# S4 convolution, router and gate on one core: kernel at 641 times, spectrum by constant matmul, order by a list

## The chip, the cores and the metric

The kernel runs on one core of a Trainium2 chip. Times are microseconds (us) of device time for one execution, and a quoted time is the median of the executions of that kernel. An execution counts as slow here when it is more than 1.5% above the fastest of its kernel. The profile of a kernel is one execution with the hardware profiler on, and its span is a little shorter than the device time. Engines: PE is TensorE's matmul, PEld its weight load, DVE is VectorE, ACT is ScalarE, POOL is GpSimd, SP is SyncE, whose queue issues most DMAs. "Clock" is the share of full speed that TensorE's clock was granted.

## The reference, cut to what matters

```python
xn = layernorm(u)                                    # [1, 2048, 512]
# S4 convolution: one kernel of 2048 taps for each of 512 channels, 128 states each
l = jnp.arange(L).astype(bfloat16)                   # <- the times are rounded
P = jnp.exp(logdA[:, :, None] * l[None, None, :])
K = jnp.einsum("dn,dnl,dn->dl", Cc, P, dB).real
y = irfft(rfft(pad(xn)) * rfft(pad(K)))[:2048] + xn * Dskip
# gate: a router picks the ONE row with the largest xn @ w_r; an FFN updates that row only
g = silu(xn + scatter(ffn(xn[row]) * sigmoid(r[row])))
out = u + y * g
```

Two facts carry the change. First, the times are rounded to bf16: 0 to 256 are exact, and each of the three octaves above has 128 values, so only 257 + 3 x 128 = 641 of the 2048 times are distinct. Second, the FFT has length 4096 and its inputs are real.

## The kernel before: the parts that matter

Its parts follow each other in the source order of a hand-written program, with hand-placed semaphore waits. The kernel K is made from powers: 65 small steps and 32 large ones for every channel, two matmuls a channel, 1024 in all, each with a 65-wide result.

```python
# 8 groups of 64 channels: sines, powers, then one matmul pair per channel
for j in range(32):
    ...
    K.op(PE, lambda t, ...: t.matmul(o_ap, lhsT=gr[:, :, dd], rhs=qr[:, :, dd], start=True, stop=False, ...
    K.op(PE, lambda t, ...: t.matmul(o_ap, lhsT=gi[:, :, dd], rhs=qi[:, :, dd], start=False, stop=True, ...
# a transposing copy on ScalarE, 16 of them
src = KT[32 * gp:32 * gp + 32, :, :].transpose([0, 2, 1])
dst = KTN[32 * q:32 * q + 32, :, 32 * gp:32 * gp + 32]
K.op(AC, lambda a, src=src, dst=dst: a.activation(out=dst, in_=src, func=ACT.Copy), sig="ktn")
```

Then K goes through the same two-stage FFT as the input, in four quarters of 128 channels. Each quarter multiplies spectra with four real products and combines them on GpSimd, inverts in two stages, and each stage change goes through DRAM.

```python
for oi, (ia, ib) in enumerate([(0, 2), (1, 3), (0, 3), (1, 2)]):
    K.op(DV, ... v.tensor_tensor(out=tb[:, oi, :], in0=ub[:, ia, :], in1=ub[:, ib, :], op=ALU.mult), ...
K.op(PO, ... g_.tensor_tensor(out=Y[:, 0, kg, :], in0=tb[:, 0, :], in1=tb[:, 1, :], op=ALU.subtract))
K.op(PO, ... g_.tensor_tensor(out=Y[:, 1, kg, :], in0=tb[:, 2, :], in1=tb[:, 3, :], op=ALU.add), sig="y")
...
for q in range(NQ):
    st_s2(q)
    st_ia(q)
    st_cd(q)
    ...
```

## Time and profile before

The time before is 629.4 us (median of four executions, 621.1 to 630.0).

The page of the profile before: the span, each engine's busy time with its share and instruction count, then 40 equal slices of the span with the busy tenths of VectorE, the granted clock and the DMA share.

```profile
span 620.8 us, 9925 instructions
PE 248.1 (40%) x3915; PEld 173.6 (28%) x3915; DVE 421.6 (68%) x1135; ACT 271.6 (44%) x405; POOL 54.3 (9%) x132
...
DVE  0989516599999899899973012709609659698725
...
PEclk9999975555755567566566555555555555555555
DMA  9920000010000000000000090499169979979293
```

No engine is full over the whole span, but VectorE is at 7 or more in most slices of the first half. The slices show phases in series: one that VectorE fills, one (slices 23 to 25) where VectorE nearly stops, and one where DMA is near 9 and VectorE swings between 0 and 9.

The same by stretch: start and end, length, busy time of the five engines (and their instruction counts), clock, DMA share, GB/s. The stretches are start, making K, gate, spectrum with inverse.

```profile
0.00:123.00 123.00, 22.06 (x215) 11.23 (x215) 73.37 (x196) 7.75 (x30) 0.20 (x4) 0.85 0.28 83
123.00:354.00 231.00, 97.82 (x1096) 66.45 (x1096) 191.05 (x515) 154.91 (x202) 0.00 (x0) 0.58 0.02 5
354.00:391.00 37.00, 1.91 (x32) 1.70 (x32) 7.08 (x15) 36.62 (x46) 0.00 (x0) 0.50 0.41 57
391.00:621.00 230.00, 126.27 (x2572) 94.17 (x2572) 150.14 (x409) 72.29 (x128) 54.11 (x128) 0.50 0.79 157
```

Making K holds VectorE for 191 of 231 us. The gate is ScalarE's alone, 36.6 of 37 us. The last stretch needs no engine for more than 150 of its 230 us: its quarters hand over from engine to engine and through DRAM.

The costliest groups of the kernel before: line, engine, operation, output and input, shapes, count, then busy time in us and the mean of one in ns.

```profile
L839 DVE TENSOR_TENSOR T<-UKB 128x128 bf16<-128x128 bf16 x256 | 65.1, 322 | 39.4 <-ACT UKB L831 38.2
...
L672 ACT ACTIVATE KTN<-KT 32x2080 bf16<-32x2080 bf16 x16 | 61.3, 3832 | 0.4
...
L883 DVE CAST C<-PB 128x512 bf16<-128x512 f32 x64 | 39.8, 684 | 18.7 <-PE PB L875 18.7
```

These are the products, the transposing copies and the evictions of the inverse's first stage, 166 us of two engines. The change removes or shrinks all three.

### The profile page before, as it was taken

To read this page: it belongs to the slowest core of one execution; us is meant where nothing else is said; L and a number is where in the kernel's file an instruction comes from. 1 tells how busy PE (TensorE), PEld (TensorE's weight loads), DVE (VectorE), ACT (ScalarE), POOL (GpSimd) and SP (SyncE) were. 2 spreads that over 40 slices of the span, in tenths; PEclk is the share of its full clock that TensorE was granted. 3 is DMA by queue.
4 is the path that set the end of the run, shared out by engine and by line. 5 is a ranking of instruction groups with operands and counts; after the bars stand their busy time and mean duration, and the time that the engine had idled before them with its cause. 6 is when DMAs were issued, how large, how long until landed. Compare 5 with 4: busy or idle time off the path is not lost.

```text
span 620.8 us, 9925 instructions
## 1 busy us (share of the span) xinstructions
PE 248.1 (40%) x3915; PEld 173.6 (28%) x3915; DVE 421.6 (68%) x1135; ACT 271.6 (44%) x405; POOL 54.3 (9%) x132
## 2 busy tenths in 40 slices
PE   0000361142632455275075010775485595534401
PEld 0000220100532224055054010773283383322201
DVE  0989516599999899899973012709609659698725
ACT  0000011374528866974962999755055055023000
POOL 0000000000000000000000000007107107126000
PEclk9999975555755567566566555555555555555555
DMA  9920000010000000000000090499169979979293
GB/s 235 366 51 0 0 1 1 3 68 0 2 0 1 1 1 1 1 2 1 1 1 1 3 133 0 113 227 183 24 186 177 184 191 186 196 195 122 119 150 71
DMA packets 93743, 49.57 MB, mean 80 GB/s; under 512 B 86688, under 2 KB 90624, under 8 KB 91776
## 3 DMA queue, kind: packets, MB, share of 16 engines
q1 hardware_dynamic: 89744, 40.50, 33.4%
q10 hardware_dynamic: 3952, 8.44, 4.1%
q8 instruction: 31, 0.51, 0.4%
q14 instruction: 16, 0.13, 0.1%
HBM read 27.96 MB, written 18.87 MB: 75 GB/s over the span
## 4 chain that ended last, share of the span: by engine, by line
DVE 31%; ACT 19%; PE 16%; issue 8%; DMA 6%; SPq 0%; POOL 0%; DVEq 0%; ACTq 0%; POOLq 0%
DVE T L839 9%; ACT KTN L672 7%; DVE C L883 6%; PE PB L775 6%; PE PB L650 3%; PE PB L652 3%; DMA D<-scr_c 2%; DVE TT L623 2%; ACT QR L556 2%; DVE EBF L570 2%; ACT QI L555 2%; DVE TT L624 2%; PE PB L867 2%; ACT PB L731 1%; ACT G L734 1%
## 5 line engine op out<-in xcount | busy, mean ns | idle before, releaser
L839 DVE TENSOR_TENSOR T<-UKB 128x128 bf16<-128x128 bf16 x256 | 65.1, 322 | 39.4 <-ACT UKB L831 38.2
L650 PE MATMUL PB<-QR,GG 128*32 128x65 bf16 x512 | 61.0, 297 | 34.9 <-DVE GG L627 34.9
L844 POOL TENSOR_TENSOR Y<-T 128x128 bf16<-128x128 bf16 x64 | 29.7, 463 | 516.0 <-DVE T L839 516.0
L550 PE MATMUL PB<-IDI,GAT 64*128 64x512 bf16 (+1 forms) x72 | 36.5, 527 | 91.2 <-ACT QR L556 78.3
L831 ACT ACTIVATE UKB<-PB 128x512 bf16<-128x512 f32 x64 | 37.7, 597 | 56.0 <-DVE T L839 30.3
L672 ACT ACTIVATE KTN<-KT 32x2080 bf16<-32x2080 bf16 x16 | 61.3, 3832 | 0.4
L652 PE MATMUL PB<-QI,GG 128*32 128x65 bf16 x512 | 60.8, 295 | 0.0
L781 ACT ACTIVATE A<-PB 128x512 bf16<-128x512 f32 x64 | 34.6, 614 | 49.0 <-PE PB L775 46.0
L883 DVE CAST C<-PB 128x512 bf16<-128x512 f32 x64 | 39.8, 684 | 18.7 <-PE PB L875 18.7
L664 ACT ACTIVATE KT<-PB 64x455 bf16<-64x455 f32 (+1 forms) x40 | 20.5, 512 | 71.6 <-PE PB L652 71.6
L825 PE MATMUL PB<-B,F 128*32 128x128 bf16 x1024 | 40.1, 307 | 27.1 <-ACT UKB L831 27.0
L556 ACT ACTIVATE QR<-PB,CONSTF 128x512 bf16<-128x512 f32 (+1 forms) x72 | 50.0, 710 | 0.0
L650 PEld LDWEIGHTS PB<-QR,GG 128*32 128x32 bf16 x512 | 37.1, 138 | 35.8 <-DVE GG L627 35.6
L555 ACT ACTIVATE QI<-PB 128x512 bf16<-128x512 f32 (+1 forms) x72 | 43.9, 610 | 4.0 <-PE PB L550 3.9
L570 DVE TENSOR_TENSOR EBF<-EBF,PIV 128x64 bf16<-128x64 bf16 (+5 forms) x48 | 41.2, 859 | 1.7
L550 PEld LDWEIGHTS PB<-IDI,GAT 64*128 64x128 bf16 x72 | 6.6, 100 | 121.4 <-ACT QR L556 107.3
L421 ACT ACT_TABLE_LOAD x1 | 1.3, 1283 | 84.7 <-DVE FT L419 84.7
L867 PE MATMUL PB<-Y,FA 32*128 32x128 bf16 x256 | 25.0, 297 | 31.9 <-DVE C L883 15.7
L652 PEld LDWEIGHTS PB<-QI,GG 128*32 128x32 bf16 x512 | 37.4, 140 | 0.0
L775 PE MATMUL PB<-XZN,CONSTB 32*64 32x128 bf16 x256 | 15.1, 309 | 54.2 <-DMA XZN<-XN 31.8
L825 PEld LDWEIGHTS PB<-B,F 128*32 128x32 bf16 x1024 | 24.8, 129 | 42.1 <-ACT UKB L831 40.8
L775 PE MATMUL PB<-KTN,CONSTB 32*64 32x128 bf16 x544 | 35.2, 308 | 0.5 <-ACT A L781 0.5
(158 smaller groups left out, 524.3 us busy)
## 6 DMA issues: line engine op xcount, KB each, us to landing
scr_a<-A SPq DMA_DIRECT2D x8, 1024.0 KB, 6.7
scr_c<-C SPq DMA_DIRECT2D x4, 2048.0 KB, 8.1
D<-scr_c SPq DMA_DIRECT2D x8, 1024.0 KB, 12.3
B<-scr_a SPq DMA_DIRECT2D x16, 264.0 KB, 4.9
B<-scr_a SPq DMA_DIRECT2D x16, 248.0 KB, 5.8
XZN<-XN SPq DMA_DIRECT2D x16, 128.0 KB, 3.8
out_dram<-X SPq DMA_DIRECT2D x16, 128.0 KB, 3.6
WG<-in_B_w_gate_dram ACTq DMA_DIRECT2D x1, 1376.0 KB, 20.0
```

The lines of the kernel that those rows point to most:

```text
L550: K.op(PE, lambda t, bank=bank, h=h, q=q, i0=i0, n=n: t.matmul(bank[:, 0:64 * n], lhsT=GAT[64 * h:64 * h + 64, q, :], rhs=IDI[64 * h:64 * ...
L555: K.op(AC, lambda a, src=src, i0=i0, n=n, qi=qi: a.activation(out=qi[:, i0:i0 + n, :], in_=src, func=ACT.Sin, scale=-1.0))
L556: K.op(AC, lambda a, src=src, i0=i0, n=n, qr=qr: a.activation(out=qr[:, i0:i0 + n, :], in_=src, func=ACT.Sin, bias=CF[:, 0:1]), sig="arguse")
L570: K.op(DV, lambda v, m=m, lv=lv: v.tensor_tensor(out=EBF[:, m:2 * m, :], in0=EBF[:, 0:m, :], in1=PIV[:, lv:lv + 1, :].to_broadcast([128, m ...
L650: K.op(PE, lambda t, o_ap=o_ap, gr=gr, qr=qr, dd=dd, gp=gp: t.matmul(o_ap, lhsT=gr[:, :, dd], rhs=qr[:, :, dd], start=True, stop=False, ti ...
L652: K.op(PE, lambda t, o_ap=o_ap, gi=gi, qi=qi, dd=dd, gp=gp: t.matmul(o_ap, lhsT=gi[:, :, dd], rhs=qi[:, :, dd], start=False, stop=True, ti ...
L672: K.op(AC, lambda a, src=src, dst=dst: a.activation(out=dst, in_=src, func=ACT.Copy), sig="ktn")
L775: K.op(PE, lambda t_, o_ap=o_ap, lhsT=lhsT, rhs=rhs, q=q, l1=l1, mi=mi, nm=len(mms): t_.matmul(o_ap, lhsT=lhsT, rhs=rhs, start=(mi == 0), ...
L825: K.op(PE, lambda t_, o_ap=o_ap, k2=k2, ro=ro, t=t, m=m, g=g: t_.matmul(o_ap, lhsT=F2[:, k2, 32 * ro:32 * ro + 32], rhs=Bt[t][par][:, m, : ...
L831: K.op(AC, lambda a_, bank=bank, kg=kg: a_.activation(out=UKB[kg % 2][:], in_=bank[:, 0:512].rearrange("p (a b) -> p a b", a=4), func=ACT. ...
L839: K.op(DV, lambda v, ub=ub, tb=tb, oi=oi, ia=ia, ib=ib: v.tensor_tensor(out=tb[:, oi, :], in0=ub[:, ia, :], in1=ub[:, ib, :], op=ALU.mult) ...
L883: K.op(DV, lambda v, g=g, kb=kb: v.tensor_copy(out=Ct[:, 16 * kb + g:16 * kb + 16:4, :], in_=PB[g][:, 0:512].rearrange("p (a b) -> p a b", ...
```

## The change

The intent has four parts.

1. **K only where it differs.** 20 large and 33 small steps for each channel cover the 641 times, so the matmuls are 33 wide instead of 65 and VectorE makes far fewer powers.
2. **Spectrum by constant matmul.** K at 640 times is five blocks of 128 rows. One constant array W, 5.2 MB, holds the sum over equal times and the transform together: 20 full-array matmuls for each group of four frequency blocks take the place of K's two-stage FFT. Time 2048, which the last four taps round to, touches only the last outputs and is added separately.
3. **Products completed in the inverse.** VectorE multiplies the input's spectrum U by K's, and a copy of U with real and imaginary halves swapped (U2S, made by DMA) by K's. The sums and signs of the complex product sit in the constants FA of the inverse. Four products and two GpSimd operations become two products, each eight times wider.
4. **Scheduled by list.** Every operation is a node with its reads, writes and an assumed duration. The builder finds dependencies from memory and banks, in the order in which nodes were created, then a list scheduler fixes each engine's order by longest remaining path. Every engine runs its fixed order.

Cut to its core (`-` before, `+` after, `...` where lines are left out; nearly the whole file is replaced):

```diff
-        for oi, (ia, ib) in enumerate([(0, 2), (1, 3), (0, 3), (1, 2)]):
-            K.op(DV, ... v.tensor_tensor(out=tb[:, oi, :], in0=ub[:, ia, :], in1=ub[:, ib, :], op=ALU.mult) ...
-        K.op(PO, ... subtract)
-        K.op(PO, ... add)
+        def spec(h, tg):                        # h: half of the channels, tg: 8 groups of 4 blocks
+            for t4 in range(4):
+                ...
+                for k in range(5):
+                    mms.append((o, W[:, t, k, :], KT2[:, h, k, :], k == 0, k == 4))
+            ...
+            g.A(lambda e: e.activation(out=ko, in_=sv, func=ACT.Copy), [ko], [sv], 1024)
+            us = (U2[:, h, 4 * tg:4 * tg + 4, :], U2S[h][:, 4 * tg:4 * tg + 4, :])
+            for x in range(2):
+                g.V(... e.tensor_tensor(out=po, in0=us[x], in1=ko, op=ALU.mult), [po], [us[x], ko], 1024, 2)
+            ...
+                    mms.append((o, FA[:, t, x, :], PAB[:, pp, x, t4, :], x == 0, x == 1))
...
+        W = place("W", [128, 32, 5, 128], BF16, o_u)               # on top of X0, AT, BT of the input FFT
+        FA = place("FA", [128, 32, 2, 128], BF16, o_u + 40960)
+        WG = place("WG", [128, 4, FF], BF16, o_u2)                 # FFN weights, on top of U2
...
+        def exps(c, after):                     # exponent arguments of part c (0..7) of K
+            src = args(0, c, c % 2)             # c % 2: PSUM banks 0,1 or banks 2,3
...
+                    bk = (2, 3, 6)[pk % 3]      # input FFT, first stage: banks 2, 3 and 6
...
+    def M(self, mms, **kw):                     # a group of matmuls as one node
+            ns += max(58.0, nn / 2.0)           # assumed duration of each
+    def dma(self, eng, pairs, **kw):
+        return self.add(eng, fns, outs, ins, 60.0 * len(pairs) + 1.3 * nd, dma=True, ...)
+    def schedule(self): ...
+            cand = [n for n in avail[e] if ready[n.i] <= t]
+            n = max(cand, key=lambda n: n.bl + n.bias)
```

## The prediction

> **What bounds the kernel now.** The page gives a span of 620.8 us: VectorE (DVE) 421.6 us busy, ScalarE 271.6, TensorE 248.1. The busy slices and the chain of waits show four phases in series. (1) 0 to 123 us: loads, layernorm, router, parameters, nearly one dependent DVE chain. (2) 123 to 354: generating the S4 kernel at 65 points, DVE about 92% busy (70.8 and 73.4 of 80 us in the table by stretch), with one stall per column quarter for the 32x2080 copies (16 x 3.83 us, ScalarE, 7% of the chain). (3) 354 to 391: the gate on ScalarE with eight reloads of activation tables at 1.28 us. (4) 391 to 621: four quarters of FFT, product, inverse, about 46 us each, in lock step; DVE works 256 products of 322 ns (65 us) and 64 evictions of 684 ns (40 us), DMA moves 256-byte packets at about 190 GB/s with 95% share, and the granted clock is 0.50.
>
> **What the change does, costed from the groups by shape.** DVE bf16 tensor_tensor: 0.29 / 0.42 / 0.69 / 1.22 us for 256 / 512 / 1024 / 2048 elements; from PSUM or in f32, 512 elements 0.69; ScalarE about 1.04 us for 1024 (estimate between 0.61 at 512 and 1.91 at 2048).
> - DVE, estimated: parameters 33, layernorm with bn_stats 26, router and gate 22, qgen 8 x 3.2 = 26, gchain 4 x 12.6 = 50, products 32 x 0.69 = 22, skip and tail 23. About 200 us against 422.
> - ScalarE: about 145 us. The KTN copies and most table loads go, and evictions become 1024 wide.
> - TensorE: 1024 small kernel matmuls at 40 to 60 ns (before: 60 ns each, 61 us for 1024), 320 + 128 full-array N=256 matmuls for the spectrum and the inverse, about 250 others. About 170 us. The Trainium skill, "TensorE: Matmul & The Clock Gate", Part 1, says a sustained burst of some 3.4 us raises the clock from 1.2 to 2.4 GHz; this trace agrees in so far as the clock drops to 0.50 in sparse stretches and reaches only 0.63 in generation bursts. I expect the dense spectrum phase mostly warm: 28 matmuls x 110 ns, 3.1 us a step, 16 steps, 50 us; cold would add about 40.
> - DMA: 7.3 MB of new constants and a 4 MB swap copy; they wait until the input FFT frees its buffers. "DMA: Bandwidth & Descriptors", Specifications, gives about 358 GB/s per core from HBM; the trace shows 358 at 10 to 30 us. At 300, about 38 us, mostly hidden under generation.
> - The list schedule overlaps layernorm, FFT and router with generation.
>
> **Critical path.** Start 10 us; DVE work before the second half's K: about 157 us, plus 5 to 10% gaps and semaphores; last kernel matmuls and the turn through DRAM 18: K complete near 205. TensorE between 150 and 245 carries the last generation (31), the gate (10) and both halves' spectra (50), so the last inverse ends near 245. Last turn through DRAM 13, tail 9, store 5: about 268 us.
>
> **Predicted: 268 us, 80% range 238 to 305.** Faster by over 2%: 0.98; within: 0.01; slower: 0.01.
>
> **What would show it.** DVE about 200 us busy and above 80% in slices up to about 190 us; no 3.8 us copies; granted clock near 1 in the spectrum phase; spectrum steps 3 to 4 us; constants landed before 165 us; last 25 us DMA turn and tail.
>
> **What would make it wrong.** A cold clock in the spectrum phase (+20 to 40); the static order of the list missing real durations, so engines stall behind waits (+30); constants or swap copies late because buffers overlay (+20); generation finishing sooner through better overlap (-25).

## The result, and the profile after

The time after is 304.85 us, median of four executions (303.2, 299.18, and two slow by the rule above, 306.54 and 306.49). Ratios in this text are the mean time of one kernel's fast runs over that of the other's of the same rounds, so not quite the ratio of the medians. Here it is 0.480, with a 95% interval of 0.474 to 0.487; the interval is wide because only two executions are fast. The kernel is 2.1 times as fast. The prediction had the direction, and its centre of 268 us was 37 us too low. The result lies inside the range by 0.15 us (304.85 against 305): its two slow executions, 306.5, lie outside, and the mean of its two fast ones is 301.2. That it fell inside is in part luck.

The page of the profile after, the same lines as before.

```profile
span 301.4 us, 4934 instructions
PE 159.4 (53%) x2067; PEld 98.3 (33%) x2067; DVE 171.7 (57%) x437; ACT 141.5 (47%) x158; POOL 0.2 (0%) x4
...
DVE  1699599999999992479650000030144446356073
...
PEclk9999999999995555855875799659789999975555
DMA  8999700000000002086899959999856649837925
```

VectorE works for 172 us instead of 422, and that is 28 us less than predicted. Yet the span is longer than predicted, so the loss is in waiting. VectorE's slices 22 to 28 (158 to 211 us) are almost empty, while DMA is mostly at 9. Read the clock row with care at the start: in this trace it has no record before 84.6 us (79.4 in the kernel before) and then shows full speed. But matmuls of 256 columns at 23.8, 41.9 and 46.2 us come 213 ns apart, against 109 ns at 87.5 us, so TensorE ran at about half speed there, and the 1.00 of the first stretch below is not a measurement.

The stretches of the kernel after, the same columns.

```profile
0.00:75.00 75.00, 17.98 (x92) 9.03 (x92) 62.69 (x192) 26.32 (x32) 0.20 (x4) 1.00 0.52 125
75.00:140.00 65.00, 33.14 (x754) 19.87 (x754) 53.06 (x148) 42.20 (x55) 0.00 (x0) 0.68 0.18 64
140.00:187.00 47.00, 28.40 (x634) 20.46 (x634) 12.84 (x26) 29.66 (x29) 0.00 (x0) 0.79 0.98 216
187.00:215.00 28.00, 14.41 (x86) 9.89 (x85) 2.88 (x5) 8.39 (x8) 0.00 (x0) 0.74 1.00 255
215.00:269.00 54.00, 50.97 (x375) 35.75 (x375) 24.34 (x39) 34.80 (x35) 0.00 (x0) 0.91 0.66 156
269.00:301.40 32.40, 14.49 (x132) 3.29 (x128) 15.88 (x30) 0.15 (x1) 0.00 (x0) 0.55 0.69 146
```

From 140 to 215 us no engine is busy for more than 43 of 75 us, and the DMA share is about 1. Before that, from 75 to 140, the DMA stands almost still at 0.18. The transfers came late and all at once.

What became of the costly groups: the products are 32 operations of about 690 ns (the sixteen that read U are shown, the others read the swap copies); the transposing copies are gone, and what replaces them is a strided eviction, KT; the kernel matmuls are still 1024, as before, but half as wide.

```profile
L1037 DVE TENSOR_TENSOR PAB<-U_50,K2T 128x1024 bf16<-128x1024 bf16 x16 | 11.1, 692 | 57.2 <-PE PB L184 37.0
...
L184 PE MATMUL PB<-QQ,GG 128*20 128x33 bf16 x1024 | 20.5, 249 | 17.0 <-DVE GG L764 9.3
L805 ACT ACTIVATE KT<-PB 128x264 bf16<-128x264 f32 x16 | 21.7, 1355 | 14.9 <-PE PB L184 14.4
```

The chain that ended last, followed back from the end (start us, length us, engine and what it did), cut to the pieces that tell the story; all matmuls of the kernel after carry the line of one helper, L184, so they are told apart by their operands.

```profile
139.56 3.85 DMA scr_a<-AT
...
148.15 13.55 DMA BT<-scr_a
...
187.04 27.97 DMA FA<-c_fa
215.06 38.99 PE PB L184 x308
...
276.74 10.04 DMA DD_117<-scr_z
```

Read it from the bottom. The dense spectrum phase starts at 215.06, when the constants FA land after 28 us under way. FA was issued at 187.04, because its memory was the input FFT's buffer BT, and the last matmul that reads BT starts at 186.7. BT was loaded late because AT, the first stage's result, was complete only at 139.56. And AT is late for a reason that its own history shows. The evictions of that stage (count, min/median/max ns, first and last start in us):

```profile
L971 ACT ACTIVATE AT<-PB x32: 572/597/932, 50.3 to 138.9; 128x512 bf16<-128x512 f32 x32
```

32 evictions of 0.6 us need 19 us of ScalarE; they were spread over 89 us, though the normalized input was complete at about 74. ScalarE in that time, in order (start, busy us, line, operation, count, idle before and its releaser):

```profile
70.96 0.60 ACT L971 ACTIVATE AT<-PB 128x512 bf16<-128x512 f32 x1 [6.97 <-DVE XN_49 L867]
82.84 2.80 ACT L805 ACTIVATE KT<-PB 128x264 bf16<-128x264 f32 x2 [11.29 <-PE PB L184]
...
99.92 1.94 ACT L697 ACTIVATE EE<-PB 128x1024 bf16<-128x1024 f32 x2 [4.79 <-PE PB L184]
...
108.31 1.41 ACT L971 ACTIVATE AT<-PB 128x512 bf16<-128x512 f32 x2
```

ScalarE had time: it idled 11.3 us at one place. But between 71.6 and 108.3 it evicted nothing of the FFT. The exponentials (EE) of the second half of K stand in between. They read their arguments from PSUM, half of them from banks 2 and 3; the FFT's first stage comes later in the source and writes banks 2 and 3, so it had to wait for them, and they in turn wait for the sines of the first half, so that activation tables change seldom. The count fits: in the source the stage's first 16 groups of matmuls take banks 2, 3 and 6 in turn, so five of them write bank 6, and five evictions, no more, came by 71.6 us. Theory: this bank order, not any engine's work, delays the FFT, and through the shared memory the constants.

### The profile page after: what moved, and what is told of

The parts are those of the page before. It is cut to its first block, busy times and chain, and to the rows that moved or that the text cites. A ratio compares the mean times of both kernels' runs of the same rounds, so it can differ in the third digit from the quotient of the medians.

```text
span 301.4 us, 4934 instructions
## 1 busy us (share of the span) xinstructions
PE 159.4 (53%) x2067; PEld 98.3 (33%) x2067; DVE 171.7 (57%) x437; ACT 141.5 (47%) x158; POOL 0.2 (0%) x4
## 4 chain that ended last, share of the span: by engine, by line
DVE 30%; PE 29%; DMA 21%; ACT 12%; SPq 4%; issue 2%; ACTq 0%
PE PB L184 29%; DMA FA<-c_fa 9%; DVE TT L760 5%; DMA BT<-scr_a 4%; SPq L198 4%; DMA DD_117<-scr_z 3%; DVE JNK L874 3%; DMA LD_66<-in_A_log_dt_dram 3%; ACT EE L697 2%; ACT U_50 L997 2%; DVE QQ L719 2%; DVE QQ L718 2%; DVE GG L762 2%; ACT AT L971 1%; DVE GG L764 1%
## 5 line engine op out<-in xcount | busy, mean ns | idle before, releaser
L184 PE MATMUL PB<-XN_49,CB 32*64 32x512 bf16 (+1 forms) x97 | 29.2, 549 | 39.1 <-ACT AT L971 22.0
L184 PE MATMUL PB<-KT_51,W 128*128 128x256 bf16 x320 | 42.3, 294 | 7.9 <-ACT K2T L1033 5.7
L184 PE MATMUL PB<-CB,AD 128*128 128x256 bf16 (+1 forms) x96 | 19.3, 362 | 38.6 <-DVE AD L650 21.7
L184 PEld LDWEIGHTS PB<-KT_51,W 128*128 128x128 bf16 x320 | 33.2, 105 | 15.3 <-ACT K2T L1033 6.6
L971 ACT ACTIVATE AT<-PB 128x512 bf16<-128x512 f32 x32 | 18.1, 632 | 28.4 <-DVE XN_49 L867 17.5
L184 PE MATMUL PB<-QQ,GG 128*20 128x33 bf16 x1024 | 20.5, 249 | 17.0 <-DVE GG L764 9.3
L805 ACT ACTIVATE KT<-PB 128x264 bf16<-128x264 f32 x16 | 21.7, 1355 | 14.9 <-PE PB L184 14.4
L1033 ACT ACTIVATE K2T<-PB 128x1024 bf16<-128x1024 f32 x16 | 16.2, 1022 | 20.2 <-PE PB L184 11.2
L1047 ACT ACTIVATE ZT<-PB 128x1024 bf16<-128x1024 f32 x16 | 16.4, 1024 | 18.0 <-PE PB L184 16.5
L184 PEld LDWEIGHTS PB<-CB,AD 128*128 128x128 bf16 x96 | 9.6, 130 | 46.3 <-DVE AD L650 21.9
L184 PEld LDWEIGHTS PB<-QQ,GG 128*20 128x20 bf16 x1024 | 17.7, 125 | 20.6 <-DVE GG L764 10.1
L184 PEld LDWEIGHTS PB<-XN_49,CB 32*64 32x64 bf16 (+1 forms) x97 | 6.3, 114 | 55.1 <-ACT AT L971 28.4
L184 PE MATMUL PB<-PAB,FA 128*128 128x256 bf16 x128 | 19.2, 300 | 6.2 <-DMA FA<-c_fa 5.7
L760 DVE TENSOR_TENSOR TT<-GG,ZB 128x512 bf16<-128x512 bf16 (+2 forms) x48 | 21.6, 485 | 0.3
L184 PEld LDWEIGHTS PB<-PAB,FA 128*128 128x128 bf16 x128 | 13.0, 106 | 10.4 <-DMA FA<-c_fa 6.0
L184 PE MATMUL PB<-BT,F2T 128*128 128x256 bf16 (+1 forms) x70 | 10.7, 306 | 10.1 <-DMA BT<-scr_a 6.5
L859 DVE BATCH_NORM_STATS2 ST<-X_78 128x6 f32<-128x512 bf16 x16 | 10.7, 686 | 5.6 <-DMA X_78<-in_A_u_dram 5.5
## 6 DMA issues: line engine op xcount, KB each, us to landing
W<-c_w ACTq DMA_DIRECT2D x4, 1280.0 KB, 11.3
```

What stands on the lines that cost most here:

```text
L184: fns.append(lambda e, o=o, l=l, r=r, st=st, sp=sp, tp=tp: e.matmul(o, lhsT=l, rhs=r, start=st, stop=sp, tile_position=tp, skip_group_chec ...
L760: g.V(lambda e, zb=zb, o=o: e.tensor_tensor(out=o, in0=src, in1=zb, op=ALU.mult), [o], [src, zs], 256 * m, 2)
L805: g.A(lambda e, src=src, dst=dst: e.activation(out=dst, in_=src, func=ACT.Copy), [dst], [src], 264)
L859: g.V(lambda e, b=b: e.bn_stats(ST[:, b, :], X0[:, b, :]), [ST[:, b, :]], [X0[:, b, :]], 512)
L971: g.A(lambda e, o=o, bk=bk: e.activation(out=o, in_=PB[:, bk, :], func=ACT.Copy), [o], [PB[:, bk, :]], 512)
L1033: g.A(lambda e: e.activation(out=ko, in_=sv, func=ACT.Copy), [ko], [sv], 1024)
```

## The experiments

The rival theories were: (B) the bank order; (C) the list's assumed durations are wrong, so its order is poor (by its formula each issue of a quarter of W, 5120 runs at 1.3 ns, holds ScalarE for 6.7 us, and that of FA for 10.7, while the trace shows 0.3 to 1.1 us for ScalarE's issues of W and FA); (F) the layout is at fault, because FA sits on the memory that is freed last; (S) the swap copies crowd FA out; (W) less work, not order, is what matters. Kernels ran beside runs of the kernel before, 629 to 630 us each time; the kernel after was not timed again, and is compared through the ratios. Its own ratio is uncertain by 1.3%, since only two of its executions are fast, so a gain of 2 to 4% over it (e2, e3, e4) is known to about one point only. Every run below is correct except where said, and the times are medians of four executions.

### e1: the exponent arguments of the second half on banks 0 and 1 only

```diff
-            src = args(0, c, c % 2)
+            src = args(0, c, c % 2 if c < 4 else 0)
```

> One edit: the second half's exponent arguments all use PSUM banks 0 and 1, so banks 2 and 3, in which the input FFT's first stage is also written, are free from about 45 us. Theory (a false bank dependency made the input side late: in the changed kernel those exponentials end at 102 us, the first-stage evictions run from 108 to 139 us, and FA therefore lands only at 215 us): first-stage evictions end before 90 us, FA lands at least 20 us earlier than 215, time 270 to 285 us against 303. Rival A (TensorE's fixed order, blocked behind generation and the router, made it late, whatever the banks): evictions still end after 120 us, time within 8 us of 303. Rival B (the constants and the swap copy are simply too many bytes once they start): the evictions end early but FA's landing follows by less than 10 us, time above 293.

Measured: 260.7 us, ratio 0.413 (0.410 to 0.415). That is 14% below the kernel after, and below the range that theory B gave, so its size was underestimated. The same view of the evictions, and three pieces of the chain of waits of this kernel:

```profile
L971 ACT ACTIVATE AT<-PB x32: 588/652/740, 43.3 to 61.8; 128x512 bf16<-128x512 f32 x32
```

```profile
107.03 5.84 PE PB L184 x15
...
152.78 12.95 DMA U2S<-U
...
166.51 17.14 PE PB L184 x140
```

The evictions now take 19 us instead of 89 and end 77 us earlier. FA is issued at 146.7 instead of 187.0 and takes 9.4 us instead of 28.0. Work is unchanged (VectorE 172.4 us, TensorE 165.2). The gain is smaller than 77 us because other things then come last: the second stage of the FFT starts at 115.4, behind the FFN in TensorE's fixed order (the piece at 107.03 holds the FFN's last matmuls). By the source the stage's output U2 lies on the FFN's weights, and every second group of it writes banks 6 and 7, of which the router and the FFN use 7 too; which of the two overlaps put the FFN first no run separates. Then the inverse waits for the swap copy of U2.

### e2: other durations in the list, most of them nearer to the trace

```diff
-            ns += max(58.0, nn / 2.0)
+            ns += max(22.0, nn / 2.0)
...
-        return self.add(eng, fns, outs, ins, 60.0 * len(pairs) + 1.3 * nd, dma=True, ...)
+        return self.add(eng, fns, outs, ins, 450.0 * len(pairs), dma=True, ...)
...
-                g.A(... func=ACT.Copy), [dst], [src], 264)
+                g.A(... func=ACT.Copy), [dst], [src], 1200)
```

> Only the durations that the list scheduler works with are corrected to measured ones: a DMA issue 0.45 us per copy instead of up to 13 us for the constants, the strided kernel eviction 1.35 us class, a small kernel matmul 22 ns instead of 58. The work itself is the same. Theory (false bank dependency first, wrong durations second): first-stage evictions still cannot use banks 2 and 3 before about 100 us, FA lands between 200 and 215, the gate moves out of the last 45 us, time 288 to 300. Rival A (wrong durations in the list are the main cause of the missed estimate): time below 280.

Measured: 290.5 us, ratio 0.462 (0.460 to 0.464). Theory C is worth about 4% (0.4617 over 0.4803), as expected, and is not the main cause: the evictions still end at 126.5 us and FA lands at 194, a little before the expected 200 to 215. The new durations are not nearer to the trace throughout: a group of four loads of BT counts 1.8 us where the old list had 5.6, and the trace of the kernel after has 21 us for eight loads, about 10.5 for four.

### e3: FA on the memory that is freed first

```diff
-        W = place("W", [128, 32, 5, 128], BF16, o_u)
-        FA = place("FA", [128, 32, 2, 128], BF16, o_u + 40960)
+        FA = place("FA", [128, 32, 2, 128], BF16, o_u)
+        W = place("W", [128, 32, 5, 128], BF16, o_u + 16384)
```

(and FA's load is listed before W's)

> FA takes the memory that is free first (that of the first FFT stage), W moves behind it and is loaded by quarters as before. Nothing else changes. Theory (the last wait before the dense spectrum phase is FA, because it lies on the memory that the input FFT frees last): FA lands before 180 us, the first inverse starts near 195 to 205 instead of 215 when the first quarter of W and the swap copy are there, time 285 to 297. Rival (the phase is paced by the bytes of W, FA and the swap together): the first inverse still starts after 210, time 298 to 306.

Measured: 294.5 us, ratio 0.468 (0.466 to 0.469). FA is issued at 143.1, 44 us earlier, and the first inverse starts at 194.1 instead of 215.1. But the time falls only by some 8 us. A write-back of the first half's result (scr_z, 203.6 to 217.7) held the chain for 14 us before the last inverse, which ends at 253 instead of 268; and gate steps, which run from 247 to 270, were left for after it, so that from there to the end it takes 40.4 us instead of 33.4. The layout is worth 3%, and is not the main cause.

### e4: no swap copies (wrong)

```diff
-        for h in range(2):
-            g.dma(SP, [(U2S[h][0:64, :, :], U2[64:128, h, :, :]), (U2S[h][64:128, :, :], U2[0:64, h, :, :])])
...
-            us = (U2[:, h, 4 * tg:4 * tg + 4, :], U2S[h][:, 4 * tg:4 * tg + 4, :])
+            us = (U2[:, h, 4 * tg:4 * tg + 4, :], U2[:, h, 4 * tg:4 * tg + 4, :])
```

> Wrong result on purpose: the 4 MB on-chip copy that swaps real and imaginary halves is left out and the second product reads the unswapped spectrum, so the output is wrong. The rest is the same, in a newly listed order. Theory (FA starts at 187 because its memory comes free then, and takes 28 us for 2 MB because it shares the DMA engines with the copy and with the kernel's turn through DRAM): FA takes 12 to 18 us, lands near 200 to 205, time 288 to 296. Rival B (bytes set the time): time below 285. Rival C (the swap copy costs nothing): time within 4 us of 303.

Measured: 295.5 us, ratio 0.469 (0.467 to 0.470); the result is wrong, as intended (relative error 0.030). FA is still issued at 185.1, but without the copies it needs 10.3 us to land, less than the expected 12 to 18 (kernel, DMA, count, KB, median us to landing):

```profile
FA<-c_fa ACTq DMA_DIRECT2D x1, 2048.0 KB, 10.3
```

So 18 of FA's 28 us went with the copies. This agrees with the Trainium skill, "DMA: Bandwidth & Descriptors", Issuing engines are not separate DMA queues: transfers started by different engines run on the same 16 DMA engines and interleave. FA was issued by ScalarE, the copies by SyncE. Leaving the copies out saves only 2%: the lateness of the issue stays.

### e5: each engine in source order

```diff
-            cand = [n for n in avail[e] if ready[n.i] <= t]
-            n = max(cand, key=lambda n: n.bl + n.bias)
+            n = next(n for n in avail[e] if n.i == seqs[e][len(self.order[e])])
```

> The same instructions as the changed kernel, but every engine issues them in the order in which the program text makes them, instead of the list's order (the waits are derived in the same way). It parts the gain of the change into less work and overlap. Theory (both matter: the work of VectorE fell from 422 to 172 us, and the list overlaps the input side with generation): 370 to 430 us, clearly faster than 629 and clearly slower than 303. Rival A (the gain is nearly all less work, the list's order adds little): below 330. Rival B (without the overlap there is little gain): above 500.

Measured: 434.9 us, ratio 0.690 (0.688 to 0.693), a little above the theory's range.

```profile
PE 186.2 (43%) x2067; PEld 106.5 (25%) x2067; DVE 183.3 (42%) x437; ACT 140.4 (32%) x157; POOL 0.2 (0%) x4
```

The same operations in source order keep no engine busy for half of the time. Against this order, 629 - 435 = 194 us of the gain come from less work, and some 130 us (435 to 305) from the list. That split holds for this one source order, which nobody wrote to be run as it stands.

### e6: e1 and e2 together

> The bank edit of the first experiment together with the corrected durations of the second. Theory (after the bank edit the rest of the lag is order: in the run with the bank edit six of the eight gate steps run alone between 210 and 235 us after the last full spectrum steps, and the FFN holds up the input's second stage until 107 us): the gates move into gaps, time 240 to 252 against 260. Rival (the corrected durations only matter while the bank dependency is there, or not at all): 256 to 264.

Measured: 267.4 us, ratio 0.425 (0.422 to 0.427): slower than e1 alone by 7 us, and outside every range given. A step of my reasoning failed: two changes that each help did not add. The chain shows what it met:

```profile
135.82 22.14 DMA U2S<-U
```

The new durations brought W, FA and both swap copies under way at once. In this kernel a quarter of W takes 19.3 us in the median and FA 15.3 (7.1 and 9.4 in e1); the swap copy that the first inverse waits for takes 22.1, against 12.95 in e1. But that copy landed at 158.0, earlier than the 165.7 of e1, so contention alone does not explain the loss. TensorE, in fixed order, stood before the gate's first matmuls until 159.3, because VectorE had queued a copy that they need behind a product that waited for the swap copy; then 15 us of gate and spectrum matmuls came ahead of the first inverse, which started at 174.1, not 166.5. The last inverse is later by as much (234.2 against 226.6). That order and contention together make the 7 us is argued from these waits; no run shows either alone.

### e7: e1, e2 and e3 together

> The sixth run's edits and FA in the memory that is free first. Theory: after the bank edit FA is issued at 147 us and no matmul waits for it any more; what the first inverse waits for is the swap copy (landing at 166 us). So FA in front gains less than the 8 us that it gained alone: 236 to 248, within 6 us of the sixth run. Rival (FA still is the last wait): 10 us or more below the sixth run.

Measured: 254.2 us, ratio 0.404 (0.402 to 0.406). 13 us below e6, which meets the rival's mark of 10 or more: with the bank order gone, FA's place matters more than it did alone. FA is issued at 74.1 and out of the way of the others: a swap copy takes 12.7 us in the median instead of 19.0, a quarter of W 8.0 instead of 19.3. The range for the theory was missed by 6 us at its upper end. The second stage of the FFT starts its first group at 98.0, the second only at 110.8 and the third at 123.5, with the FFN's products (103.7 to 122.0) among them, and the last inverse ends at 220.5.

### e8: e7, and the router with the FFN ahead in the list

```diff
+        g.boost = 60000.0            # added to the rank of each node until it is set back
         for b in range(16):
             g.V(lambda e, b=b: e.tensor_tensor_reduce(out=JNK[:], in0=XN0[:, b, :], in1=WRB[:], ...
...
+        g.boost = 0.0
         gchain(0)
```

> The seventh run's edits, and the router's and FFN's instructions get a higher priority in the list, since the FFN's weights lie where the input spectrum U2 goes. Theory (after the bank edit the input's second stage waits from about 86 us, when its data is there, to 107 us for the FFN): the second stage starts before 95 us and the time falls to 225 to 240. Rival (generation of the second half, bound by VectorE, is by then the last wait): second stage earlier, but time within 3 us of the seventh run.

Measured: 248.2 us, ratio 0.394 (0.394 to 0.395), the fastest. The FFN's update is ready at 87.6 instead of 124.7 us. The second stage starts at 96.6 instead of 98.0 (before 95 was expected), its third group at 100.2 instead of 123.5, but its eighth at 127.2 instead of 135.3: most of the lead is lost on the way. The total falls by 6 us: less than the theory gave, and more than the rival's 3. In TensorE's order, kernel matmuls that wait for VectorE until 93.3 now stand before the second stage, and more matmuls of K, with waits for ScalarE, among its later groups (idle 1.1 to 3.3 us at a time). So the making of K, and no longer the FFN, seems to hold it; no run tests that.

### e9: the bank order removed by the other side

From the kernel after; the FFT's first stage leaves banks 2 and 3, and the exponentials stay where they were:

```diff
-                    bk = (2, 3, 6)[pk % 3]
+                    bk = 6
```

> A second, different way to remove the same false dependency: the second half's exponents stay on banks 2 and 3 as in the changed kernel, and the input FFT's first stage instead writes only bank 6, one bank without rotation. Theory (the shared banks 2 and 3 are the cause): the first-stage evictions end before 105 us although they now have one bank instead of three, and the time is 262 to 280. Rival (the gain of the first experiment came from some other effect of the new listing): evictions still end after 125 us, time above 292.

Measured: 274.7 us, ratio 0.435 (0.433 to 0.437). The evictions end just past the expected 105:

```profile
L971 ACT ACTIVATE AT<-PB x32: 569/597/947, 41.6 to 105.1; 128x512 bf16<-128x512 f32 x32
```

Two of three banks were taken away from the stage, and the kernel is 9% faster than after. A shortage of banks or of ScalarE could not do that; an order between users of banks 2 and 3 can. With one bank each matmul waits for the eviction before it, so the evictions take longer than in e1 and gain less. This is the second, independent route to theory B.

### e10: e8, and the gate's steps ahead in the list

```diff
+        g.boost = 20000.0
         for k in range(8):
             gate_step(k)
+        g.boost = 0.0
```

> The eighth run's edits, and the gate steps get a higher priority. In the eighth run six of eight gate steps fall after the last spectrum product (203 to 222 us), between inverses that run at the cold rate, 1.9 us instead of 1.04 for eight matmuls. Theory (the late gates hold the last inverses and so the last turn through DRAM): the last inverse ends 5 to 9 us earlier than at 215.6, time 238 to 244 against 248. Rival (the gates only use time that is needed anyway, moving them early pushes the spectrum back by as much): within 2 us of 248.

Measured: 254.4 us, ratio 0.403 (0.401 to 0.405): slower than e8 by 6 us. The theory fell. SyncE's queue in both kernels, e10 first (start, us, line, DMA, count):

```profile
219.93 1.87 SPq L199 DMA_DIRECT2D out_dram<-XR  x4
221.89 0.42 SPq L199 DMA_DIRECT2D scr_z<-ZT  x1
224.17 1.84 SPq L199 DMA_DIRECT2D out_dram<-XR  x4
226.42 4.32 SPq L199 DMA_DIRECT2D DD<-scr_z  x4
```

```profile
219.76 4.00 SPq L199 DMA_DIRECT2D DD<-scr_z  x4
228.15 15.61 SPq L199 DMA_DIRECT2D out_dram<-XR  x16
```

The load DD, on which the end depends, is issued 6.7 us later. About 3 us of that is the spectrum itself: its last inverse is at 218.8 us, against 215.6 in e8, because the gates now stand among its steps. The rest is the queue: with the gates done early, results of the first half were ready to be stored, and eight stores stand ahead of DD, four of them ahead of the last write-back scr_z that DD reads. In e8 all stores come after it. A gap was filled that was not on the path.

### e11: e8 without the new durations

> The eighth run's edits without the corrected durations (bank edit, FA in front, router first, the list's own durations). The sixth run was 7 us slower than the first, which it should have improved on by correcting durations, so the sign of that correction is open. Theory (truer durations help once the banks, the FA memory and the router are mended): 252 to 262, slower than the eighth run's 248. Rival (the correction is harmful or of no use throughout): 240 to 248.

Measured: 264.0 us, ratio 0.419 (0.416 to 0.422), 16 us slower than e8 and just above the expected range. The new durations help here by 16 us, help by about 12 us in e2 (by the ratios), and hurt by 7 us in e6. Durations that are mostly nearer to the trace are not a gain that one may count on: they select another order, and its worth depends on what else is in the list. Why the sign changes stays open; that some of the new durations, BT's above all, are further from the trace than the old ones may be part of it, which no run tests.

## Why the prediction was right or wrong

**Right: the direction and the main terms of work.** VectorE was predicted at about 200 us and measured at 171.7, ScalarE at about 145 and 141.5, TensorE at about 170 and 159.4. The 3.8 us copies are gone. But the mark "above 80% in slices up to about 190 us" was missed: VectorE is almost empty from 158 us on, because it waits.

**Right: the spectrum phase is dense and warm.** 28 matmuls were predicted at 3.1 us a step. TensorE in the kernel after, in order (start, busy us, then operation, shapes and count):

```profile
224.31 1.04 PE L184 MATMUL PB<-PAB,FA 128*128 128x256 bf16 x8
225.19 2.35 PE L184 MATMUL PB<-KT_51,W 128*128 128x256 bf16 x20
227.37 1.04 PE L184 MATMUL PB<-PAB,FA 128*128 128x256 bf16 x8
```

One step is 227.37 - 224.31 = 3.06 us, or 109 ns a matmul. The Trainium skill, "TensorE: Matmul & The Clock Gate", Back-to-back issue gap, gives N/2.4 + 2.5 ns for the gap of an isolated warm matmul, from which we estimate 109 ns at N = 256, and says that a real stream can run below it at large N; this stream runs at 109. When the phase starts at 215.06 after a wait of 5.7 us, the same eight matmuls take 1.89 us and not 1.04. The first warm matmul comes 6.1 us later; after an earlier wait of 5.7 us, at 198.70, it came 5.3 us later. Part 1 of that page has a window of about 3.4 us that runs freely and does not start with the kernel, so up to two windows, 6.8 us by our estimate, may pass; both waits fit that. The matmuls then ran warm from 221.2 to 266.2, 45 of the phase's 54 us.

**Wrong: "mostly hidden under generation", with the mark "constants landed before 165 us".** This is the step that failed. W, FA and the swap copies were to hide under the making of K. The DMA share from 75 to 140 us, the generation's main stretch, was 0.18; they came from 144 on, and FA landed at 215. The prediction costed the volume (38 us at 300 GB/s) and knew that the buffers overlay the input FFT's, but did not ask when that FFT would end. It took for granted that "the list schedule overlaps layernorm, FFT and router with generation". The list could not: by creation order and by bank, the FFT's first stage depended on the exponentials of the second half of K. e1 and e9 remove that dependency in two ways, one line each, and save 14% and 9%. The layout (e3), the durations (e2) and the swap copies (e4) are worth 2 to 4% each from the kernel after, each uncertain by about one point. The prediction had named this risk ("constants or swap copies late because buffers overlay (+20)") beside the list's static order (+30), both inside its range, but had put neither into its centre. So the range held by its listed risks and by 0.15 us, while the path behind its centre was not the one that the kernel took.

**How 37 us came about.** The prediction let the last inverse end at 245; it ended at 268, 23 us later. The turn through DRAM and the tail take 33.4 us from there to the end of the span, against 27 in the prediction, 6 us more, in which the load of DD lands 19 us after the last inverse instead of 13, with TensorE at half its clock. The prediction's own terms sum to 245 + 27 = 272, and it wrote 268: 4 us. The remaining 2 us are device time outside the span. The sum is 35 us, for the execution profiled at 303.2 us; the median is 2 us above that.

**Mis-sized the other way: "K complete near 205".** VectorE's work for K ended at 156.4 us. The prediction had VectorE 28 us too high and 1024 kernel matmuls at 40 to 60 ns; they took 20 ns (20.5 us in all). The last eviction of K still came at 190.5, because TensorE's fixed order put the last parts of K behind the second stage of the FFT, which waited for BT (they ended at 170.9), and ScalarE's fixed order put their last eviction behind the evictions of that stage. So an early gain was swallowed by the same late FFT. e1 collected part of it: VectorE is busy for 95 of its first 107 us, and the last eviction of K ends at 161.0.

**The wording of the risks.** "A cold clock in the spectrum phase (+20 to 40)" did not happen: the clock is 0.91 from 215 to 269 (0.5 until 221.1, then full). "Generation finishing sooner (-25)" did, and was not worth anything while the FFT was late.

**What stays open.** Why the new durations help in e2 and e8 and hurt in e6; whether U2's memory or bank 7 puts the FFN before the second stage; and how much of the last 30 us, the turn through DRAM at a clock of about 0.5, can be taken away. The fastest version, e8, is at 248.2 us: VectorE works 127 of its first 155 us, TensorE 57.6 of the next 60.6, and the tail takes the last 30.6.

## What to carry to other kernels

A scheduler is bound by the dependencies that it is given, and those come from reused memory, banks and the order of the source as well as from data; before counting an overlap, find for each buffer who used its bank and its bytes before, and when that user ends. A term of DMA is not costed by its volume alone: its earliest start is the release of the memory it lands on, and when several waiting transfers are released together one of them can take three times as long as when less else is under way (FA: 28 us against 9.4 in e1). Test an order of operations by its parts and in combination, since corrections that help alone may cost time together.

## What the Trainium skill lacked or had wrong

- "TensorE: Matmul & The Clock Gate", Wait — 56ns, not 53.3ns?, says that start-to-start never drops below about 25 ns. Here 64 kernel matmuls of 33 columns with 20-column weights, spread over the four column strips of the array, take 1.27 us, 20 ns each, and 1024 take 20.5 us. They start in fours within about 10 ns, a new four about every 65 ns. That fits "TensorEngine Tiling (Array Packing)", Key Properties, by which different tiles can load weights and multiply in parallel, but neither page gives a figure for a stream of them with new weights for every matmul.
- "ScalarE: Activation LUTs" gives 0.833 ns per element for all functions. Contiguous evictions agree (1024 elements 1022 ns, 512 elements 597 ns: 0.83 ns per further element). The eviction of K, 264 elements that are written 128 bytes apart, takes 1355 ns, which is more than the contiguous one of 1024. "SBUF — State Buffer", Door 1, names a penalty for each access to a new 16-byte line, without a figure for ScalarE.
- No page that I found gives a time for which a DMA issue holds SyncE or ScalarE. In the kernel after, a free issue on SyncE took 0.32 us (AT's store), but the eight loads of BT, with W under way, took 2.7 us each in the median and up to 4.9, 21 us for eight, during which the queue can issue nothing else.
- "TensorE: Matmul & The Clock Gate", Part 1, says that what is issued in the first 3.4 us or so runs at half clock and everything after at full clock. As a budget that is too short here: in the kernel after it took 5.3 and 6.1 us from the end of a wait (198.70 and 215.06) to the first matmul at full speed. The freely running window of the same page allows for that, up to two windows by our estimate.
